# Natural query order out of the softmax, and one 128-row store per unit, in a sliding-window attention and feed-forward kernel

## The chip, the cores and the metric

The kernel runs on one core of a Trainium2 chip. The metric is device time in microseconds (us) of one execution; lower is better. Each kernel was run several times beside the kernel before on the same chip. "Span" is the time from the first to the last instruction in a trace; the device time is 1.7 us longer than the span in every run that lists both.

## The reference, cut to what matters

```python
def _attn_ref(q, k, v):                  # q, k, v: (8, 8, 576, 64)
    scores = scale * np.matmul(q, k.transpose(0, 1, 3, 2))
    mask = np.abs(pos[:, None] - pos[None, :]) <= 32
    ...                                  # softmax over the masked scores
    return np.matmul(attn, v)

def _moe_ref(x, w_in, w_out):            # x: (4608, 512), w_in: (512, 2048)
    h = x @ w_in
    g = h * (1.0 / (1.0 + np.exp(-1.702 * h)))
    return g @ w_out
```

4608 token rows are worked on in 36 units of 128 rows; the rows of a unit are two blocks of 64 queries.

## The kernel before

Queries and keys are loaded four rows to a partition. After the transposition the four rows are told apart by an index `j`, and the scores of a block of 64 queries have their columns in the order (j, s), where the natural row is 4 s + j. Before, that order is kept through the exponential, the mask, the value product and both feed-forward layers, and the store undoes it. Only the last unit is put in order earlier, since its rows wrap around.

```python
    def scores(self, u):
        ...                                              # matmuls into sc[eo], columns (j s)
        for eo in range(2):
            if u < self.NU - 1:
                nc.scalar.activation(p[:, eo], sc[eo], AF.Exp, scale=self.scale)
            else:                                        # last unit: permuted on the write side
                nc.scalar.activation(p[:, eo].rearrange("k h (s j) -> k h j s", j=JT),
                                     sc[eo].rearrange("k h (j s) -> k h j s", j=JT), AF.Exp, scale=self.scale)

    def layer2(self, u, quarter, kind="o", eng=None):
        ...                                              # 16 matmuls into o_ps over four calls
        if quarter == 3:
            o_sb = self.work.tile([128, self.DM], F32, name="o_sb", tag="o_sb", bufs=4)
            self.cast(eng or nc.vector, o_sb, o_ps)
            row = 128 * u + 32
            for blk in range(2):
                nc.sync.dma_start(self.out[row + 64 * blk:row + 64 * blk + 64, :].rearrange("(s j) f -> j s f", j=JT),
                                  o_sb[64 * blk:64 * blk + 64])
```

In the steady state a window of the schedule takes two units: their scores, 24 layer-2 matmuls of earlier units (with key transposes between them), their value matmuls, 8 more layer-2 matmuls and 64 layer-1 matmuls.

The softmax here doesn't subtract the row's maximum and nothing guards it: scores larger than these inputs give would overflow.

## Time and profile before

| | before |
|---|---|
| device time, median of 4 runs | 322.66 us (321.83 to 325.1) |
| span of the profiled run | 319.5 us |
| TensorE busy | 307.0 us |
| last matmul's stretch ends | 314.5 us |
| output stores, units 0 to 34 | 70 transfers of 128 KB, 2 per unit |

The prediction below shows the page's main lines. Three more views matter; the prediction did not use the lines below, and the result shows that it should have. The first is the list of waits ("engine line waited for: us in total, times, longest us"), the second the chain that ended last, in order of time (start us, us, what), around 172 us:

```profile
PE tp L154 <- issue: 2.0, 1, 2.0
...
PE o_ps L319 <- issue: 0.7, 1, 0.7
```

The third view is that of the transfers in the window from 164 to 175 us: the busy share of the 16 transfer engines in 40 slices of 0.275 us, in tenths, and the queue that brings instructions.

```profile
DMA  9999969999999999999232222223399978029999
...
q8 instruction: 1, 0.02, 2.4%
```

From 169 us on the share falls to 2 or 3 tenths, four or so of 16 engines. And one instruction fetch of 16 KB takes 2.4% of 16 engines' 11 us, 4.2 us. The mean over the whole run is 1.2 us (30 fetches, 0.7% of 16 times 319.5 us).

### The profile page before, as it was taken

Reading aid. Unit: us, or ns where it says so; the run is one execution under the profiler, and the core shown is the slowest. Engines: PE = TensorE matmul, PEld = TensorE weight load, DVE = VectorE, ACT = ScalarE, POOL = GpSimd, SP = SyncE. Lnnn points to the kernel's source line nnn. Section 1 sums busy time; section 2 is a strip of 40 time slices with the busy share of each in tenths; the row PEclk is TensorE's granted clock in tenths of the full one; section 3 lists DMA queues with packets and bytes.
Section 4 is the critical chain, followed back from the end, with each engine's and each line's share of the span. In section 5 each row is a group of like instructions: output and inputs, shape, how many; then the busy total and the mean of one; then the engine's idle time right before and its main releaser. Section 6 shows DMA issues by size and latency. Waiting matters only on the chain.

```text
span 319.5 us, 8946 instructions
## 1 busy us (share of the span) xinstructions
PE 307.0 (96%) x3856; PEld 209.4 (66%) x3856; DVE 139.1 (44%) x422; ACT 189.2 (59%) x299; POOL 71.8 (22%) x105
## 2 busy tenths in 40 slices
PE   7979999999999999999997999999999999999993
PEld 4658655756757574858573858585858485857763
DVE  2463058557672807371727254535452516170001
ACT  3565454784857574757574666666666676775330
POOL 8983555414241203220302011101000000000000
PEclk9999999999999999999999999999999999999998
DMA  8999999989999999999199919490934031505103
GB/s 140 144 175 205 195 189 183 211 145 137 142 78 128 129 111 103 178 141 108 27 146 117 144 42 115 88 113 22 133 69 87 20 81 28 77 10 89 35 18 82
DMA packets 92543, 35.05 MB, mean 110 GB/s; under 512 B 65240, under 2 KB 88024, under 8 KB 92504
## 3 DMA queue, kind: packets, MB, share of 16 engines
q0 software_dynamic: 61248, 18.22, 70.8%
q1 hardware_dynamic: 31160, 16.19, 32.8%
q8 instruction: 30, 0.49, 0.7%
q10 hardware_dynamic: 96, 0.07, 0.1%
q14 instruction: 9, 0.07, 0.1%
HBM read 36.96 MB, written 9.44 MB: 145 GB/s over the span
## 4 chain that ended last, share of the span: by engine, by line
PE 88%; POOL 3%; DMA 3%; DVE 2%; issue 2%; ACT 1%; POOLq 0%; ACTq 0%
PE h_ps L308 39%; PE o_ps L319 37%; PE pv L269 3%; PE sc L232 3%; DMA w_in_sb<-in_moe_w_in_dram 3%; PE tp L154 2%; PE tp L157 1%; POOL ve L137 1%; PE o_ps L340 1%; DVE p L253 1%; DVE p L258 1%; DVE x L281 1%; POOL ks L131 1%; POOL qs L131 0%; POOL edge L206 0%
## 5 line engine op out<-in xcount | busy, mean ns | idle before, releaser
L308 PE MATMUL h_ps<-xT,w_in_sb 128*128 128x256 bf16 x1152 | 130.9, 273 | 0.6 <-DMA w_in_sb<-in_moe_w_in_dram 0.6
L319 PE MATMUL o_ps<-w_out_sb,g 128*128 128x512 bf16 x560 | 130.0, 380 | 0.7 <-issue 0.7
L308 PEld LDWEIGHTS <-w_in_sb 128*128 128x128 bf16 x1152 | 111.6, 98 | 17.6 <-DMA w_in_sb<-in_moe_w_in_dram 0.9
L310 ACT ACTIVATE g<-h_ps 128x512 bf16<-128x512 f32 x144 | 86.0, 597 | 47.5 <-PE h_ps L308 47.2
L319 PEld LDWEIGHTS <-g 128*128 128x128 bf16 x560 | 51.5, 98 | 55.9 <-issue 1.2
L103 DVE COPY kT<-tp 128x512 bf16<-128x512 bf16 (+2 forms) x45 | 26.0, 595 | 92.5 <-PE tp L154 69.5
L137 POOL DMA_DIRECT2D ve<-in_v_dram x40 | 33.7, 849 | 139.1 <-PE pv L269 100.9
L253 DVE TENSOR_TENSOR p<-p,mask 128x512 bf16<-128x512 bf16 x70 | 26.4, 422 | 27.1 <-ACT p L238 26.4
L238 ACT ACTIVATE p<-sc 128x512 bf16<-128x512 f32 x70 | 36.3, 603 | 2.6 <-PE sc L232 2.3
L103 ACT COPY o_sb<-o_ps 128x512 f32<-128x512 f32 x15 | 8.8, 585 | 46.3 <-PE o_ps L319 46.3
L281 DVE TENSOR_TENSOR x<-pv,rec 128x256 bf16<-128x256 f32 x72 | 30.6, 425 | 2.5
L103 DVE COPY o_sb<-o_ps 128x512 f32<-128x512 f32 x20 | 13.6, 686 | 24.4 <-PE o_ps L319 24.4
L280 DVE RECIPROCAL rec<-pv 128x4 f32<-128x4 f32 x72 | 12.6, 175 | 17.9 <-PE pv L269 17.9
L238 ACT ACT_TABLE_LOAD x15 | 19.2, 1283 | 0.3
L348 ACT ACT_TABLE_LOAD x14 | 18.0, 1283 | 0.3
L269 PEld LDWEIGHTS <-p 128*64 128x64 bf16 x576 | 11.2, 110 | 9.8 <-issue 6.6
L103 ACT COPY qT<-tp 128x512 bf16<-128x512 bf16 (+1 forms) x17 | 9.6, 572 | 11.9 <-PE tp L157 11.0
L232 PEld LDWEIGHTS <-kT 64*64 64x64 bf16 x1152 | 11.6, 107 | 5.4 <-issue 5.0
L269 PE MATMUL pv<-ve,p 128*64 128x65 bf16 x288 | 13.9, 196 | 1.0 <-DVE p L253 0.8
L232 PE MATMUL sc<-qT,kT 64*64 64x64 bf16 x1152 | 14.3, 194 | 0.4 <-ACT qT L103 0.2
L269 PE MATMUL pv<-vo,p 128*64 128x65 bf16 x288 | 13.9, 196 | 0.2 <-DVE p L258 0.2
L131 POOL DMA_DIRECT2D qs<-in_q_dram x17 | 12.4, 731 | 6.1 <-DMA ks<-in_k_dram 1.8
(56 smaller groups left out, 143.0 us busy)
## 6 DMA issues: line engine op xcount, KB each, us to landing
out_dram<-o_sb SPq DMA_DIRECT2D x70, 128.0 KB
ve<-in_v_dram POOLq DMA_DIRECT2D x32, 128.0 KB, 9.6
w_in_sb<-in_moe_w_in_dram POOLq DMA_DIRECT2D x4, 512.0 KB, 11.0
w_out_sb<-in_moe_w_out_dram POOLq DMA_DIRECT2D x4, 512.0 KB, 12.4
ks<-in_k_dram POOLq DMA_DIRECT2D x2, 448.0 KB, 11.6
qs<-in_q_dram POOLq DMA_DIRECT2D x2, 448.0 KB
ks<-in_k_dram POOLq DMA_DIRECT2D x3, 256.0 KB, 12.1
qs<-in_q_dram POOLq DMA_DIRECT2D x3, 256.0 KB, 22.1
```

The lines of the kernel that those rows point to most:

```text
L103: (eng.copy if eng is self.nc.scalar else eng.tensor_copy)(out, in_)
L131: self.nc.gpsimd.dma_start(self.stage[key][off // JT:(off + m) // JT, lo:hi, :], src[b, lo:hi, s:s + m, :].rearrange("h (p j) d -> p h (j ...
L137: self.nc.gpsimd.dma_start(self.ve[m % NV][off:off + n, :, :self.D], self.v[b, :, s:s + n, :].rearrange("h s d -> s h d"))
L232: nc.tensor.matmul(sc[eo][lo:lo + 64, 2 * hp + blk, :], self.kT[r, hp, at:at + 64], self.qT[r, JT * hp:JT * hp + JT, q0:q0 + 16], start=(n ...
L238: nc.scalar.activation(p[:, eo], sc[eo], AF.Exp, scale=self.scale)
L253: self.nc.vector.tensor_mul(pv, pv, msk.to_broadcast([128, 4, 2, SQ]))
L269: nc.tensor.matmul(acc[half][blk * 64:blk * 64 + 64, hh, :], p[:, h % 2, h // 2 * 2 + blk, :], vt[:, h, :D + 1], start=(hh == 0), stop=(hh ...
L281: nc.vector.tensor_mul(x[:, hs, :], acc[half][:, :, :D], rec[:, hs, :].to_broadcast([128, 4, D]))
L308: nc.tensor.matmul(hps[:, i, :], self.w_in_sb[:, kr, ff * 128:(ff + 1) * 128], self.xT[t][:, kr, :], start=(i == 0 and kr == 0), stop=(i = ...
L310: nc.scalar.activation(self.g[t][:, 2 * d:2 * d + 2, :], hps, AF.Gelu_apprx_sigmoid)
L319: nc.tensor.matmul(o_ps, self.g[t][:, ff, s * 128:(s + 1) * 128], self.w_out_sb[:, ff, :], start=(ff == 0), stop=(ff == self.NFF - 1))
L348: self.nc.scalar.activation(self.spark, self.spark, AF.Gelu_apprx_sigmoid)
```

## The change

Its intent: put the queries in natural order once, in the exponential, by reading PSUM with a stride of 16 fp32 elements and writing contiguously. Then masks are in natural order, the last unit needs no special case, and a unit's result leaves in one transfer of 128 contiguous rows.

```diff
-            if u < self.NU - 1:
-                nc.scalar.activation(p[:, eo], sc[eo], AF.Exp, scale=self.scale)
-            else:
-                nc.scalar.activation(p[:, eo].rearrange("k h (s j) -> k h j s", j=JT),
-                                     sc[eo].rearrange("k h (j s) -> k h j s", j=JT), AF.Exp, scale=self.scale)
+            nc.scalar.activation(p[:, eo].rearrange("k h (s j) -> k h s j", j=JT),
+                                 sc[eo].rearrange("k h (j s) -> k h s j", j=JT), AF.Exp, scale=self.scale)
 ...                                     # band(): the last unit's four half products are gone
-            row = 128 * u + 32
-            for blk in range(2):
-                nc.sync.dma_start(self.out[row + 64 * blk:row + 64 * blk + 64, :].rearrange("(s j) f -> j s f", j=JT),
-                                  o_sb[64 * blk:64 * blk + 64])
+            nc.sync.dma_start(self.out[128 * u + 32:128 * u + 160, :], o_sb)
 ...                                     # masks: built with pattern [[0, 2], [-sign, 64]], cut in contiguous columns
```

## The prediction

> **What bounds the kernel now.** I read the page's head first, then the groups of instructions, the clock, the chain of waits and finally the timeline of single stretches.
>
> ```profile
> span 319.5 us, 8946 instructions
> ...
> PE 307.0 (96%) x3856; PEld 209.4 (66%) x3856; DVE 139.1 (44%) x422; ACT 189.2 (59%) x299; POOL 71.8 (22%) x105
> ...
> PE 88%; POOL 3%; DMA 3%; DVE 2%; issue 2%; ACT 1%; POOLq 0%; ACTq 0%
> PE h_ps L308 39%; PE o_ps L319 37%; PE pv L269 3%; PE sc L232 3%; DMA w_in_sb<-in_moe_w_in_dram 3%; PE tp L154 2%; PE tp L157 1%; POOL ve L137 1%; PE o_ps L340 1%; DVE p L253 1%; DVE p L258 1%; DVE x L281 1%; POOL ks L131 1%; POOL qs L131 0%; POOL edge L206 0%
> ```
>
> TensorE is busy 96% and carries 88% of the chain that ends last; the two feed-forward layers alone are 76% of it. A busy TensorE need not be at its peak, so I checked the pace: in the chain a full layer-1 stage is 64 matmuls of 256 columns in 6.99 us, 109 ns each, and 24 layer-2 matmuls of 512 columns take 5.18 us, 216 ns each. Twice the columns cost twice the time, at a mean granted clock of 0.997, so these stretches have no hidden slack. The change touches no matmul. It can only win in the places where TensorE stands still: the head (before about 26 us), the last attention window (near 284 us) and the tail after the last matmul (314.5 to 319.5 us).
>
> The exponentials, the second group that matters, look like this:
>
> ```profile
> L238 ACT ACTIVATE p<-sc 128x512 bf16<-128x512 f32 x70 | 36.3, 603 | 2.6 <-PE sc L232 2.3
> L253 DVE TENSOR_TENSOR p<-p,mask 128x512 bf16<-128x512 bf16 x70 | 26.4, 422 | 27.1 <-ACT p L238 26.4
> L240 ACT ACTIVATE p<-sc 128x512 bf16<-128x512 f32 x2 | 2.5, 1374 | 0.0
> L258 DVE TENSOR_TENSOR p<-p,mask 128x256 bf16<-128x256 bf16 x4 | 2.2, 602 | 0.8 <-ACT p L240 0.8
> ```
>
> Line 240 is the last unit's exponential, which already puts its queries in natural order, but the other way round: it reads PSUM in memory order and writes single bf16 elements 8 bytes apart. The reader should see that the permuted write costs 1374 against 603 ns. The question of this case is whether the permuted read does too.
>
> **What the Trainium skill says.** "ScalarE: Activation LUTs", section "What ACT_TABLE_LOAD costs", gives 186 ns + 0.833 ns per element for an activation with immediate scale, so 613 ns for 512 elements; the trace has 603, which agrees. It says nothing there on strides. "SBUF — State Buffer" (the "cachelines" note) says that SBUF has 16-byte and PSUM 8-byte lines, that accesses which cross to a new line pay, and that a non-contiguous PSUM pattern slows matmuls. For PSUM reads by the other engines this trace disagrees:
>
> ```profile
> L103 DVE COPY kT<-tp 128x512 bf16<-128x512 bf16 x36 | 24.7, 689 | 92.5 <-PE tp L154 69.5 <-PE tp L157 23.0
> L103 DVE COPY o_sb<-o_ps 128x512 f32<-128x512 f32 x20 | 13.6, 686 | 24.4 <-PE o_ps L319 24.4
> L103 ACT COPY qT<-tp 128x512 bf16<-128x512 bf16 x16 | 9.2, 584 | 11.9 <-PE tp L157 11.0 <-PE tp L154 0.9
> L103 ACT COPY qT<-tp 128x256 bf16<-128x256 bf16 x1 | 0.4, 378 | 0.0
> ```
>
> The kT copies on VectorE read PSUM in inner runs of four elements 256 bytes apart, and take 689 ns for 512 elements; a contiguous fp32 read of 512 takes 686. The single 256-element qT copy on ScalarE (the edge block) reads every fourth bf16, a new 8-byte line each time; (584 − 378) / 256 = 0.80 ns per element, the contiguous rate. So a strided PSUM read was free on both engines, although neither case is fp32 at 64-byte steps on ScalarE, which is what the change does.
>
> "DMA: Bandwidth & Descriptors", section "Why a DMA increments its semaphore by 16 and not by 1", states that a transfer is split over the largest k up to 16 that divides the slowest dimension of both sides. The stores of before have 4 (j) on the DRAM side and 64 rows on the SBUF side, so k = 4; a store of 128 rows would have k = 16. The trace agrees with k = 4, as the tail shows:
>
> ```profile
> 312.00:312.50 0.50, 0.50 (x7) 0.44 (x6) 0.00 (x0) 0.00 (x0) 0.00 (x0) 1.00 0.25 98
> ...
> 315.50:315.75 0.25, 0.00 (x0) 0.00 (x0) 0.00 (x0) 0.00 (x0) 0.00 (x0) 1.00 0.86 148
> 315.75:316.00 0.25, 0.00 (x0) 0.00 (x0) 0.00 (x0) 0.00 (x0) 0.00 (x0) 1.00 0.45 111
> 316.00:316.25 0.25, 0.00 (x0) 0.00 (x0) 0.00 (x0) 0.00 (x0) 0.00 (x0) 1.00 0.82 209
> 316.25:316.50 0.25, 0.00 (x0) 0.00 (x0) 0.00 (x0) 0.00 (x0) 0.00 (x0) 1.00 0.75 234
> 316.50:316.75 0.25, 0.00 (x0) 0.00 (x0) 0.00 (x0) 0.00 (x0) 0.00 (x0) 1.00 0.62 209
> 316.75:317.00 0.25, 0.00 (x0) 0.00 (x0) 0.00 (x0) 0.00 (x0) 0.00 (x0) 1.00 0.38 127
> 317.00:317.25 0.25, 0.00 (x0) 0.00 (x0) 0.00 (x0) 0.00 (x0) 0.00 (x0) 1.00 0.20 66
> 317.25:317.50 0.25, 0.00 (x0) 0.00 (x0) 0.00 (x0) 0.00 (x0) 0.00 (x0) 1.00 0.12 41
> ```
>
> The last two columns are the busy share of the 16 transfer engines and GB/s. At 312.0, with unit 33's two stores alone in flight, the share is 0.25: four engines, 98 GB/s, 24.5 each.
>
> **The change part by part.**
>
> Exponentials, 70 of the 72: the read becomes fp32 at 64-byte steps, the write contiguous. From the two free strided reads above I take 603 ns as before: 0.
>
> The last unit: two exponentials of 1374 ns become two of 603, and four mask products of 602 ns become two of 422. ScalarE saves 1.5 us, VectorE 1.6 us. Nearly all of it is hidden, since 24 layer-2 matmuls (5.2 us) run meanwhile. What TensorE really loses: its value matmuls there start at 283.73 and hand over at 284.75, 1.02 us, against 252.99 to 253.62, 0.63 us, two windows earlier. The difference, 0.4 us, is the wait for the last mask product (the record has 0.3 us on the weight load). With it gone the products end about 1.5 us before they are needed: −0.4 us.
>
> Stores inside the run: 70 issues of about 537 ns become 35, some 19 us of queue time on SyncE; nobody on TensorE waits for that queue, nor for a store (the waits list has no compute engine waiting for out_dram, and no copy into o_sb waits for its four buffers). Value: 0.
>
> The tail: the last 256 columns' copy ends at 314.94; its store is issued at 315.0 and its bytes start near 316.0. Between 316.0 and 317.75 the windows add up to 0.25 × (209 + 234 + 209 + 127 + 66 + 41 + 41) = 232 KB (the last 41 is the window at 317.50, not shown), but that last store is 128 rows of 1 KB, 128 KB. The rest, about 100 KB, is unit 34's store of 256 KB, issued at 311.75 and still draining at 98 GB/s (2.7 us if alone) on its four engines, with the last store's own share for those four engines behind it. Hence the falling shares 0.38, 0.20, 0.12. Over 16 engines unit 34's bytes would take about 1.2 us at the observed 209 to 234 GB/s, be gone by about 314.5, and the last store would run from 316.0 to 316.0 + 128 KB / 220 GB/s = 316.6. Its end now is about 317.75; I take −1.1 us.
>
> The head: GpSimd's four mask selects (340 ns each) lie in its chain of issues before the first w_in load, which TensorE waits for at 20.12 us (0.6 us on the matmul, 0.9 on the weight load). They keep 64x128 elements, with one index dimension fewer. At the rate of the identity's select (287 ns for a single-dimension pattern) they would give 0.2 us together, and the transfer engines are so loaded there that half of it might arrive: −0.1 us.
>
> Sum: −0.4 − 1.1 − 0.1 = −1.6 us, 0.5% of 322.78. Predicted time 321.2 us.
>
> **The rivals.** First, the strided fp32 read is slow. For it: the skill's note on PSUM lines, and the 1374 ns of line 240. Against: the two free reads. Its size can be worked out from the slack. In the window at 231 us four exponentials run from 233.12 to 235.18, 0.49 us apart, the mask products end at 235.97, the value matmuls start at 237.28 and need the second unit's products at about 237.6. That is 1.6 us of slack, 0.4 us per exponential; up to roughly 1.0 us each the windows would hide it. At line 240's spacing of about 1.1 us they would miss by 4 × 0.6 − 1.6 = 0.8 us in each of some 14 windows, 11 us, plus 2 to 3 us in the head: about 335 us, 4% slower. If the step were only 100 ns dearer, ScalarE's total would rise by 7 us and the time by nothing.
>
> Second, the tail gain is not there: if the last store's landing is set by its fixed latency and not by the queue on four engines, only 0.5 us remain and the time is 322.3. Against it speaks the byte count above.
>
> Third, stores on four engines slow the loads and transposes that share them, so spreading them speeds the middle. The middle shows no TensorE wait for a transfer after the w_in one, so this too is worth nothing in time; it should only lower the landing times. In reverse, a store on all 16 engines stands ahead of every transpose, but for 256 KB / 16 engines, about 0.7 us at 24.5 GB/s each, against windows of slack.
>
> **Range and chances.** The baseline's own runs spread over 321.83 to 325.1, wider than the effect. With the sum between −0.3 and −2.5 us and a spread of about 1.5 us, 319.2 to 323.8 should hold 8 times in 10. Over 2% faster would need 6.5 us, more than all stalls that the change can reach: 2%. Slower by over 2% needs the first rival at nearly full size: 7%. The rest, 91%, is within 2%.
>
> **What would show it.** In the profile after: exponentials near 603 ns (right up to 700; above 1.0 us the first rival holds, with waits of TensorE on the mask products in every window); in the last window value matmuls of 0.63 us with no wait on VectorE; while a single store is in flight a share well above 0.25 and a rate above 98 GB/s; the last bytes by about 316.7 us if the last matmul stays near 314.5 us; the span about 1.6 us shorter with TensorE's busy time unchanged at 307 us. I would be wrong if the span fell without the tail shrinking, or if TensorE's idle time grew in the middle windows.

## More of the kernel before

The whole TensorE stream is straight-line code, 3856 matmuls each with its weight load.

The reader should see that TensorE, the engine that bounds this kernel, stands still for 2.0 us between the first and the second of four equal transposes, although all four have their operands.

```profile
171.73 0.63 PE pv L269 x29
172.37 0.16 PE tp L154
172.53 2.04 issue
174.56 0.34 PE tp L154 x3
```

"issue" means that the engine waited for nothing that the profile shows: no semaphore and no data.

## The result, and the profile after

| | before | after |
|---|---|---|
| device time, median of 4 runs | 322.66 us | 315.17 us (314.79 to 316.02) |
| span of the profiled run | 319.5 us | 313.3 us |
| ratio, 95% interval | | 0.9746 (0.9698 to 0.9794) |
| output stores, units 0 to 34 | 70 of 128 KB | 35 of 256 KB, 2.6 us to landing |

The ratio is the mean time of the changed kernel's fast runs over that of the kernel before's fast runs of the same rounds, so it is not quite the ratio of the medians. Executions over 1.5% slower than the fastest of the same kernel are left out of the means. The change is faster by 2.5%, outside the predicted range.

Following one place after another through the two chains of waits tells where the 6.2 us of span went:

| stretch | before | after | gained |
|---|---|---|---|
| head, to the end of the first 96-matmul stretch of layer 1 | 36.62 | 35.06 | 1.6 us |
| stall in layer 2 near 123 us | 0.8 us | none | 0.8 us |
| stall in the key transposes at 172.5 us | 2.2 us | none | 2.2 us |
| last unit's value matmuls | 1.02 us | 0.63 us | 0.4 us |
| last matmul's stretch to the end of the span | 319.5 − 314.5 | 313.3 − 309.5 | 1.2 us |

The groups that answer to those of before (mean of one in ns after the comma):

```profile
L248 DVE TENSOR_TENSOR p<-p,mask 128x512 bf16<-128x512 bf16 x72 | 27.8, 433 | 26.5 <-ACT p L236 25.8
L236 ACT ACTIVATE p<-sc 128x512 bf16<-128x512 f32 x72 | 37.3, 604 | 2.6 <-PE sc L231 2.3
```

The strided read costs nothing: 604 ns, against 603 for the contiguous one. The same place of the chain as shown of before, and the same 11 us of transfers (here from 162 to 173 us):

```profile
169.34 0.63 PE pv L259 x29
169.97 0.33 PE tp L153 x4
170.30 1.73 PE o_ps L309 x8
```

```profile
DMA  9999999999999999950499999999799996029999
...
q8 instruction: 2, 0.03, 1.4%
```

The four transposes run through without the 2 us of "issue". The long stretch at 2 tenths is gone, and two fetches take 1.4% of 16 times 11 us together, 1.2 us each on average. In the tail (windows of 0.25 us; the last two columns are the share of the transfer engines and GB/s), the last store's bytes are out in 0.7 us:

```profile
310.75:311.00 0.25, 0.00 (x0) 0.00 (x0) 0.00 (x0) 0.00 (x0) 0.00 (x0) 1.00 0.59 139
311.00:311.25 0.25, 0.00 (x0) 0.00 (x0) 0.00 (x0) 0.00 (x0) 0.00 (x0) 1.00 0.90 242
311.25:311.50 0.25, 0.00 (x0) 0.00 (x0) 0.00 (x0) 0.00 (x0) 0.00 (x0) 1.00 0.46 144
```

**A theory for the stalls.** The transfer queue called "instruction" moved 30 blocks of 16 KB in either kernel. TensorE has 7,712 matmuls and weight loads, which is 30.1 blocks of 256; so these are TensorE's own instructions, 64 bytes each. Numbering TensorE's records in the trace of before (these 7,712 and 42 others, mostly semaphore events, in order of time), the two stalls come after record 3265 and after record 4545, which are 193 + 12 × 256 and 193 + 17 × 256: both at the end of a block. The twelfth fetch began 7.9 us after TensorE had passed the block end before it (1.6 us in the changed kernel) and ended at 121.79 us, and TensorE went on at 123.35. The seventeenth took 4.20 us (1.39 in the changed kernel), ended at 173.05, and TensorE went on at 174.56. In both, TensorE resumed 1.5 us after the fetch had ended.

The Trainium skill, "Runtime: NRT & Kernel Launch", section "Instruction fetch mechanics", says that the sequencer fetches the next block of 256 instructions by a transfer while it runs the current one, and that this is mostly hidden. The block size agrees with this trace; that it is hidden does not.

Theory A: stores confined to four of the 16 transfer engines fill those engines' queues, fetches that share them come late, and TensorE starves. Its rivals: the stalls are accidents of one profile (B); the number of store transfers, or SyncE's queue time, counts (C); natural order itself pays (D).

### The profile page after: what moved, and what is told of

Its sections match the earlier page's. It is cut to its first block, busy times and chain, and to the rows that moved or that the text cites. A ratio compares the mean times of both kernels' runs of the same rounds, so it can differ in the third digit from the quotient of the medians.

```text
span 313.3 us, 8901 instructions
## 1 busy us (share of the span) xinstructions
PE 304.1 (97%) x3856; PEld 208.1 (66%) x3856; DVE 138.6 (44%) x420; ACT 187.7 (60%) x299; POOL 71.7 (23%) x105
## 4 chain that ended last, share of the span: by engine, by line
PE 93%; DVE 2%; DMA 2%; ACT 1%; POOL 1%; issue 0%; POOLq 0%
PE h_ps L298 40%; PE o_ps L309 39%; PE sc L231 4%; PE pv L259 3%; PE tp L153 2%; DMA ks<-in_k_dram 2%; PE tp L156 2%; PE o_ps L327 1%; DVE x L271 1%; DVE p L248 1%; PE junk L341 1%; PE tp L286 1%; ACT p L236 1%; ACT qT L102 0%; DVE rec L270 0%
## 5 line engine op out<-in xcount | busy, mean ns | idle before, releaser
L248 DVE TENSOR_TENSOR p<-p,mask 128x512 bf16<-128x512 bf16 x72 | 27.8, 433 | 26.5 <-ACT p L236 25.8
L236 ACT ACTIVATE p<-sc 128x512 bf16<-128x512 f32 x72 | 37.3, 604 | 2.6 <-PE sc L231 2.3
L102 DVE COPY o_sb<-o_ps 128x512 f32<-128x512 f32 x20 | 13.6, 684 | 24.8 <-PE o_ps L309 24.8
L236 ACT ACT_TABLE_LOAD x15 | 19.2, 1283 | 0.3
```

What stands on the lines that cost most here:

```text
L102: (eng.copy if eng is self.nc.scalar else eng.tensor_copy)(out, in_)
L236: nc.scalar.activation(p[:, eo].rearrange("k h (s j) -> k h s j", j=JT), sc[eo].rearrange("k h (j s) -> k h s j", j=JT), AF.Exp, scale=sel ...
L248: self.nc.vector.tensor_mul(pv, pv, msk.to_broadcast([128, 4, 2, SQ]))
```

## The experiments

### e1: the kernel before, profiled again

No edit.

> The kernel before, unchanged, for a second profile of it. Theory A (the stores' four transfer engines delay TensorE's instruction fetches): the ratio is 1.00, and the profile again has stretches of 0.5 to 2.5 us in the middle of the run where TensorE issues nothing and no semaphore is waited for, at the same places in its instruction stream (instructions 3265 and 4545, both 193 past a multiple of 256), though not always at both. Theory B (these two stalls are accidents of one profile): ratio 1.00, no such stall, and a span about 3 us below 319.5. First layer-1 matmul at 20.1 us if the head's 1.4 us belong to the change, anywhere between 18.7 and 20.5 if the head merely varies.

Measured: 325.89 us median (323.71 to 328.25), ratio 1.008 (0.998 to 1.017), span 322.4 us. The stalls are there again and longer, after the same instructions (of the weight loads no record is missing, so the place can be counted in every profile): TensorE's weight loads (start us, us, engine, line) stop after the first key transpose, for 3.0 us this time.

```profile
173.15 0.10 PEld L154 LDWEIGHTS <-kc 128*128 128x128 bf16 x1
176.21 0.24 PEld L154 LDWEIGHTS <-kc 128*128 128x128 bf16 x3 [2.96 <-issue]
```

This run also shows a second cost. The column after the five engines is TensorE's granted clock:

```profile
176.20:179.10 2.90, 2.67 (x9) 1.25 (x11) 2.23 (x8) 0.00 (x0) 0.00 (x0) 0.50 1.36 155
179.10:185.00 5.90, 5.90 (x54) 5.11 (x53) 0.36 (x2) 3.61 (x7) 0.00 (x0) 1.00 2.47 125
```

After the 3.0 us stall TensorE runs at half clock for some 3 us, layer-2 matmuls 0.43 us apart where they are 0.216 at full clock. "TensorE: Matmul & The Clock Gate", section "HAM oscillation — how this bites in real kernels", warns of idle gaps over about 3.4 us; here shorter ones were enough, but not always. Counted from the end of one matmul to the start of the next, TensorE's pauses of 2.83 us in this run, 2.94 in e10 and 3.36 in e7 were followed by 3.4 us of half clock; those of 2.04 us in the first profile and of 2.75 and 2.82 in e3 were not. The runs of the kernel before went from 320.0 to 328.3 us, those of the changed kernel from 314.7 to 317.1; stalls that vary and are sometimes followed by half clock can explain part of that scatter. The first layer-1 matmul was at 19.3 us, so the head wanders. Theory B falls.

### e2: two contiguous stores of 64 rows

```diff
-            nc.sync.dma_start(self.out[128 * u + 32:128 * u + 160, :], o_sb)
+            for r0 in (0, 64):
+                nc.sync.dma_start(self.out[128 * u + 32 + r0:128 * u + 96 + r0, :], o_sb[r0:r0 + 64])
```

> The changed kernel with two stores of 64 contiguous rows per unit in place of one of 128 (both sides divisible by 16, so 16 transfer engines each). Theory A (spread over the engines is what counts): as the changed kernel, ratio 0.975, within 0.4% of it. Rival C (the number of store transfers and the SyncE queue time counts): back towards 1.00, at least 0.985.

Measured: 315.27 us, ratio 0.9748 (0.9689 to 0.9806), span 313.1 us, no stall in the middle. Two transfers per unit in place of one cost nothing, and theory C falls.

### e3: natural order, stores on four engines

```diff
-            nc.sync.dma_start(self.out[128 * u + 32:128 * u + 160, :], o_sb)
+            for r0, n in ((0, 124), (124, 4)):
+                nc.sync.dma_start(self.out[128 * u + 32 + r0:128 * u + 32 + r0 + n, :], o_sb[r0:r0 + n])
```

The row counts come from the rule that the prediction cites from "DMA: Bandwidth & Descriptors": neither 124 nor 4 has a divisor between 4 and 16.

> The changed kernel with the stores split as 124 + 4 rows, whose row counts share no larger divisor up to 16 than 4, so that natural order is kept and four transfer engines carry all stores, 32 rows each, as before. Theory A: most of the gain is lost; the tail's 1.1 us come back and the fetch stalls too, span 317 to 320 us, ratio 0.99 to 1.00, and a TensorE stall at an instruction index of 193 + 256 n. Rival D (natural order itself is what pays): ratio 0.975.

Measured: 324.67 us, ratio 0.9958 (0.9853 to 1.0062), span 321.4 us. Two of the four runs count as slow and are left out of the ratio; the fast ones took 323.14 and 321.01 us. The ratio is as expected, the span a little over the 317 to 320 us expected. With natural order kept, all the gain that can be told from noise is gone, and theory D falls. The chain stops after the first key transpose once more:

```profile
173.93 0.16 PE tp L153
174.09 2.82 issue
176.91 0.34 PE tp L153 x3
```

The seventeenth fetch took 6.0 us here. The stall near 122 us is there too, 2.8 us long, after a fetch that began 9.2 us behind the block end before it.

### e4: the old order, stores on 16 engines

```diff
             for blk in range(2):
-                nc.sync.dma_start(self.out[row + 64 * blk:row + 64 * blk + 64, :].rearrange("(s j) f -> j s f", j=JT),
-                                  o_sb[64 * blk:64 * blk + 64])
+                for j in range(JT):
+                    at = 64 * blk + 16 * j
+                    nc.sync.dma_start(self.out[row + 64 * blk:row + 64 * blk + 64, :].rearrange("(s j) f -> j s f", j=JT)[j],
+                                      o_sb[at:at + 16])
```

> The kernel before with its old query order, each store cut in four so that every transfer has 16 rows on both sides and uses 16 engines (eight transfers of 16 rows per unit). Theory A: nearly the whole gain without the new order: ratio 0.975 to 0.985, span 313.5 to 316 us, no TensorE stall in the middle, the last unit's wait of 0.4 us still there. Rival D: ratio 1.00. Rival C: ratio over 1.00, as there are four times as many transfers.

Measured: 317.61 us, ratio 0.9831 (0.9757 to 0.9905), span 315.6 us, no stall in the middle, no fetch over 2 us after the head. Most of the gain comes without the new order. Of the 2.3 us of span that are missing to the changed kernel, 1.8 are found in this trace: the last unit's wait of 0.38 us is still there, and the tail from the last matmul on is 1.4 us longer, so no shorter than before's, with eight issues of SyncE for each unit. The last unit and the tail therefore have no part in this run's gain of 5.3 us between the means.

### e5: the changed kernel again, as the yardstick

No edit.

> The changed kernel unchanged, as the yardstick for the next runs on this chip, and a second profile of its head. All theories: 315.2 us, within 0.4%. Its first layer-1 matmul was at 18.74 us; the first profile of before had it at 20.12, a second one at 19.48. If it stands again between 18.5 and 19.3, the head's share of the gain may be real; only 0.2 us of it can be traced to the mask's selects.

Measured: 316.21 us median, mean of the six runs 316.02, ratio 0.9809 (0.9767 to 0.9851), no stall in the middle. The median is 0.3% over the first measurement's, within the band expected, and the gain is 1.9% in these rounds, where it was 2.5% in the first. The first layer-1 matmul was at 19.6 us, later than the 18.5 to 19.3 that would have spoken for a gain in the head. Over the profiles it came at 20.1, 19.3 and 18.7 us with the old masks (before, e1, e4) and at 18.6, 18.6, 19.2, 19.6, 18.8, 22.1 and 18.3 with the new ones (after, e2, e3, e5 to e8). The 1.6 us of head in the table above are therefore mostly the luck of one pair of traces, and no gain of the change in the head can be told from its scatter. The traces show where most of it comes from. Ahead of the real work TensorE runs idle matmuls of 256 columns (`keep_busy`); eight of them, first in before and then in after (start us, us):

```profile
7.88 1.89 PE L354 MATMUL junk<-idle 128*128 128x256 bf16 x8
7.66 1.05 PE L341 MATMUL junk<-idle 128*128 128x256 bf16 x8
```

In before they follow each other at 213 ns up to about 10.3 us, in after at 109 ns from about 4.3 us, as at half and full clock. The same late step to full pace, at 10 us or later, is in e5 and e7 and in no other of the ten, and these three have the latest heads (20.1, 19.6, 22.1 us).

### e6: only the last full unit's store on four engines

```diff
-            nc.sync.dma_start(self.out[128 * u + 32:128 * u + 160, :], o_sb)
+            for r0, n in ((0, 124), (124, 4)) if u == self.NU - 2 else ((0, 128),):
+                nc.sync.dma_start(self.out[128 * u + 32 + r0:128 * u + 32 + r0 + n, :], o_sb[r0:r0 + n])
```

> The changed kernel with only the last full unit's store (unit 34) on four engines (124 + 4 rows). Theory A with the tail as predicted: 1.0 to 1.3 us slower than the changed kernel of the same rounds, all of it after the last matmul (3.3 to 3.8 us from the last matmul's start to the end of the span becomes 4.6), no stall in the middle. Rival (the last store is bound by its own latency): under 0.4 us slower.

Measured: 317.10 us median, mean of six runs 317.19, so 1.2 us over e5's mean in the same rounds; no stall in the middle. From the end of TensorE's last matmul to the end of the span the trace has 5.1 us, against 3.8 in e5. The tail's part of the prediction is confirmed.

### e7: all other stores on four engines

The same edit with `u < self.NU - 2`.

> The changed kernel with all stores but unit 34's on four engines. Theory A: 3 to 8 us slower than the changed kernel, with TensorE stalls of 1 to 3 us at the same two places in its instruction stream (indices 3265 and 4545 where no record is missing, about 3252 and 4526 as counted in the second profile of before), after a fetch that came late or took over 2 us, and the tail as short as the changed kernel's.

Measured: 321.82 us median of four runs. One of them counts as slow; the three fast ones have a mean of 320.59, which is 4.6 us over e5's 316.02. The profile fell on the slow run (span 321.9 us): TensorE stalls for 3.4 us after the first key transpose, behind a fetch that took 6.0 us; the stall near 122 us did not come in this run, and the head was 2.5 us late. How much the stalls cost varies: the three fast runs are 2.1, 5.2 and 6.4 us over e5's mean, so 4.6 is a rough figure. Two others agree with it: e4 gained 5.3 us in the middle, and e3's fast runs are 6.8 us over e2's mean, 5.6 without the tail's 1.2.

### e8: all other stores on two engines

The same edit with `((0, 122), (122, 6))`, so that two engines carry 61 rows each of every unit.

> The changed kernel with all stores but unit 34's as 122 + 6 rows, so that two engines carry nearly all of each store (61 rows each). Theory A, and the fetches ride on one of the first two engines: stalls longer than with four engines, 6 to 20 us slower than the changed kernel. Theory A, and the fetches ride on the third or fourth engine or others: no stall at the two places, within 2 us of the changed kernel, unless TensorE comes to wait for a data transfer instead.

Measured: 367.56 us, ratio 1.139 (1.132 to 1.146), 51 us over e5, far more than the 6 to 20 expected. The list of waits shows longer issue stalls and something new, TensorE waiting for the transposed activations and queries themselves:

```profile
PE h_ps L298 <- DMA xT<-x: 13.6, 2, 9.0
...
PEld L298 <- issue: 11.8, 2, 7.8
...
PE sc L231 <- DMA qT<-qc: 6.0, 1, 6.0
```

So the cost grows as the same bytes are put on fewer engines, from nothing at 16 by 4.6 us at four to some 50 at two. Counting instructions divides the loss of the profile. Six gaps between weight loads of 1.8 to 5.1 us, 20 us together, lie at block ends (193 + 256 × 9, 10, 11, 12, 20 and 23, within two records); five others of 1.6 to 7.9 us, 23 us together, lie elsewhere, where the profile names the transfer or the copy of activations or queries. One fetch took 12.1 us, but three of the six stalls at block ends ended 4.7 to 11.8 us after the fetch of that block, so a late fetch fits only the other three. That stalls grow with two engines fits fetches that ride on one of those two, but the records do not name the engine, so this is not shown.

### e9: natural order made on the write side

```diff
-            nc.scalar.activation(p[:, eo].rearrange("k h (s j) -> k h s j", j=JT),
-                                 sc[eo].rearrange("k h (j s) -> k h s j", j=JT), AF.Exp, scale=self.scale)
+            nc.scalar.activation(p[:, eo].rearrange("k h (s j) -> k h j s", j=JT),
+                                 sc[eo].rearrange("k h (j s) -> k h j s", j=JT), AF.Exp, scale=self.scale)
```

> The changed kernel with the natural order made on the write side of the exponential in all 36 units (PSUM read in memory order, single bf16 elements written 8 bytes apart), as the kernel before did it for its last unit only. The prediction's first rival, by its own working: 1374 ns for one exponential, about 1.1 us apart, 0.8 us of wait on the mask products in each of some 14 windows and 2 to 3 us in the head, so 11 to 14 us slower than the changed kernel, 326 to 330 us. If the windows hide more than worked out: under 320 us.

Measured: 333.31 us, ratio 1.036 (1.030 to 1.042). The exponential (ns min/median/max) and TensorE's wait (us in total, times, longest us):

```profile
L236 ACT ACTIVATE p<-sc x72: 1295/1390/1419, 12.1 to 295.2; 128x512 bf16<-128x512 f32 x72
```

```profile
PE pv L259 <- DVE p L248: 8.6, 14, 0.8
```

TensorE stands still in each of the twelve steady windows for 0.78 to 1.0 us, as worked out (0.8); that is 10 us. The miss is in the early part, where some 7 us were lost to the changed kernel's trace instead of 2 to 3: 3 us before the first long layer-1 stretch, where the granted clock of this trace is 0.50 from 13.6 to 20.4 us, and four gaps of 0.8 to 1.1 us between 52 and 77 us. The slack argument holds where the windows are regular, and the side on which the stride lies decides: 604 ns for the read, 1390 for the write.

### e10: 32 more instructions ahead in TensorE's stream

```diff
-        self.keep_busy(12)
+        self.keep_busy(28)
```

> The kernel before with 16 more idle matmuls at the very start of TensorE's stream (32 instructions more), which delay the head by 2 to 4 us. Theory A (the stalls are late instruction fetches, bound to a multiple of 256 in the stream): the long stall near 172 us, which came after the first of four key transposes in four of four profiles with four-engine stores, now comes 32 instructions earlier in the program, in the midst of the 32 value matmuls ahead of these transposes. Rival (something at that place in the program holds TensorE): the stall stays after the first key transpose.

Measured: one run, 323.7 us. The weight loads ahead of the key transposes:

```profile
175.57 0.36 PEld L269 LDWEIGHTS <-p 128*64 128x64 bf16 x17 [0.42 <-issue]
176.69 0.33 PEld L269 LDWEIGHTS <-p 128*64 128x64 bf16 x15 [0.75 <-issue]
177.06 0.23 PEld L154 LDWEIGHTS <-kc 128*128 128x128 bf16 x4
```

The stall left the transposes and now cuts the value matmuls at the seventeenth of 32 weight loads, 32 instructions earlier in the program, as theory A says. (The gap of 0.42 ahead of the first line is there in every window.) So the place is bound to the count of instructions and not to the transposes. The cause of this one stall is less clear: it is shorter, 0.8 us between starts, and the seventeenth fetch had ended at 173.04 us, 2.8 us before TensorE stopped. The 16 more matmuls did not delay the head as expected; its first layer-1 matmul was at 19.8 us. In this run another stall of 3.1 us lies in the scores at 117 us, and the profile puts 2.9 us there down to the transfer of the transposed queries: with stores on four engines that transfer comes late too.

## Why the prediction was wrong

- **The strided read is free: right.** 604 ns, and the arithmetic from two other strided reads carried over to fp32 at 64-byte steps. Rival 1 did not come, and e9 showed that its size for a steady window (0.8 us) was right.
- **The last unit, −0.4 us: right.** Its value matmuls went from 1.02 to 0.63 us.
- **The tail, −1.1 us: right.** The two traces give 1.2 and e6, with that store alone on four engines, gives 1.2.
- **The head, −0.1 us: not resolved.** The selects went from 340 to 288 ns, as taken, but the head scatters from 18.3 to 22.1 us at the first layer-1 matmul.
- **"Stores inside the run", value 0: wrong, and this is the step that failed.** The prediction reasoned that "nobody on TensorE waits for that queue, nor for a store", and put aside its third rival because "The middle shows no TensorE wait for a transfer after the w_in one". It looked for waits on a semaphore. TensorE also waits for its own instructions, which a transfer queue brings; such a wait shows as "issue". The chain of waits it quoted had "issue 2%", and the list of waits had 2.0 and 0.7 us in the middle of the run. e7 measured this term at 4.6 us, roughly. With it the parts add up: 4.6 + 1.2 + 0.4 = 6.2 us, where the fast runs of before in the rounds of e5 to e7 have a mean of 321.92 us, 5.9 over the changed kernel's.
- **The chances: too narrow for the same reason.** The gain that was called "more than all stalls that the change can reach" was measured against the stalls with a named releaser. The scatter of the kernel before was taken as noise of measurement; at least in part it was the effect, since the stalls vary and some are followed by a stretch at half clock. How large that part is was not measured.
- **A sign that failed: "TensorE's busy time unchanged at 307 us".** It was 304.1. Of the 2.9 us, 2.3 lie in the first 12 us, where the idle matmuls of before ran at half pace for longer (see e5); that is no effect that any run here ties to the change.

Left open: what exactly TensorE waits for at a block end. In the profiles taken here, 14 gaps of more than 0.75 us lie at block ends; ten of them end 1.2 to 1.9 us after the fetch of that block, the other four (three in e8, one in e10) 3.6 us or more after it. That few-engine stores bring the stalls is shown by e3, e4 and e7, and that they sit at block ends by the counts and by e10; that the fetch itself is what comes late fits most of them, not all. Also open: which transfer engine brings TensorE's instructions, and why the stalls hit these two blocks. Both of these fetches fall where loads and query transposes crowd the engines as well (the sixteen engines are at 9 tenths just ahead of 169 us in the kernel before), but no run took those loads away.

## What to carry to other kernels

Look at how many transfer engines a store really uses (a share of 0.25 with one store in flight is four of 16) and give it a row count on both sides that 16 divides, even when no engine waits for the store. On a long straight-line kernel, read "issue" stalls of the bounding engine as possible late instruction fetches, and check whether they recur at a fixed distance in the instruction stream. If an order must be changed in an exponential out of PSUM, put the stride on the read (604 ns here, against 1390 with the stride on the write).

## What the Trainium skill lacked or had wrong

- "Runtime: NRT & Kernel Launch", "Instruction fetch mechanics", calls the crossing of a block "mostly hidden". Here TensorE stopped for 0.8 and 2.2 us in one profile and 3.0 us in another, at multiples of 256 instructions plus 193, and the stores on four engines that bring such stalls cost 4.6 us on average (e7). In these three TensorE went on 1.3 to 1.6 us after the fetch's last byte. A fetch took 0.9 to 2.0 us in the profiles with stores on 16 engines, and up to 6.0 us with stores on four.
- No page says that stores confined to few transfer engines can delay instruction fetches (6.0 us for one in e3 and e7); the rule of "DMA: Bandwidth & Descriptors" for the number of engines gives the row counts that avoid it.
- "SBUF — State Buffer", the note on cachelines, names matmuls and GpSimd, not ScalarE, and gives 8 bf16 as a step that is free. A strided fp32 read of PSUM at 64-byte steps took 604 ns where the contiguous one took 603; a bf16 write to SBUF at steps of 4 elements (8 bytes) took 1390 ns (e9).
